# One transposing transfer of q issued from ScalarE's queue in place of SP's, in an attention and gated feed-forward kernel

## The chip, the cores and the metric

The kernel runs on one core of a Trainium2 chip. The engines that compute are TensorE (PE, whose weight loads are PEld), VectorE (DVE), ScalarE (ACT) and GpSimd (POOL); SyncE (SP) only issues transfers. Sixteen DMA engines move the data of all queues. The metric is the device time of one execution in microseconds (us), as the median of several.

## What is computed

For each of 8 batches and 8 heads, an attention without a score matrix, then a gated feed-forward over all 4608 tokens:

```
q_s = softmax(q, over the 64 channels)          # q, k, v: 8 x 8 x 576 x 64, float32
k_s = softmax(k, over the 576 positions)
kv  = k_s^T v                                    # 64 x 64 per head
x   = q_s kv                                     # all heads side by side: 4608 x 512
out = ((x w1) * (x w2)) w3 w_out                 # w1, w2: 512 x 1024; w3: 1024 x 1024; w_out: 1024 x 512
```

## The kernel before

Each batch is one round of attention, which prepares a chunk of 512 tokens of x, and one round of the feed-forward on that chunk; the 64 tokens left over of each batch make a ninth chunk. w3 and w_out are folded at the start into one matrix, W3O. The rounds are interleaved: while PE works on the feed-forward of chunk b, the other engines prepare the attention of the batches behind it.

Nothing orders the work at run time but semaphores. Each engine, and each engine's queue of transfers, takes its instructions in the order in which the program issued them, and that order is one long list of step names, `ORDER` (lines 77 to 164), written out by hand for all engines together. `Plan.run` (48 to 72) goes through it and calls each step's function; `attention` (521 to 797) and `chunk` define the steps, with the engine of each, what it needs and the time by which it was planned. A step's name ends in the batch and a part.

The steps that matter here:

- q of a batch comes in two parts, `PARTS` (298): p = 0 holds four blocks of 64 tokens, p = 1 five. For each part the softmax runs as `qmx` (maximum, DVE, L620), `qsub` (L625), `qexp` (ACT, L633), `qsm` (sum, DVE, L638), `qeps`, `qrc`, and `qn` (L657), which writes the normalized q in f16 into the tile `en`.
- `en` must be transposed into `qT` before PE can multiply it. Batch 0 and part 1 of batch 1 do that on PE (`qt`, L672, with evictions `qT`, L366). The others do it by a transfer, `qd` (L678 to 680): a transposing DMA from `en` to `qT`. `DMATP` (354) adds part 0 of batch 1 to these, so `qd.1.0` is the first such transfer of the run.
- `xm` (L705) multiplies `qT` by the kv matrix on PE; `xm.1.0` needs `qd.1.0`. `xs` evicts it to x (L370), and `up` (L851), `down` (L873) are the feed-forward.
- k of a batch: `kmx` (maximum, DVE, L532), `cba`, `cbx` (four small copies on ACT that exchange rows between groups of partitions, L545), `cb` (DVE, L549 and L551), `ksub` (L555), `kexp` (ACT, L563). `vc` casts v to f16 (L366). `kv` (PE, L580) needs both parts of `kexp` and of `vc`; `kve`, `kvr`, `kv2` finish it.

The loads come by two queues. Those of the weights and of the first batches are issued by POOL (`LOADS`, 252), those from q of batch 2 on by SP (`LATE`, 259; L450). The first of SP's late loads, `q.2`, waits until the load of w1's last part has landed. SP also issues all stores (L913, L1072) but for a few near the end, which ACT issues.

Around the change the order is, engine by engine:

- SP: `q.2`, `qd.1.0`, `v.2`, `k.3`, the stores of chunk 0.
- ACT: `bs.0.0.3`, `W3O.6`, `cbx.2`, `vc.1.1`, `kexp.1.0`, `vc.1.0`, `bs.0.1.3`, `os.0.1`, `kve.1`.
- POOL: `qn.1.0` comes before `ksub.1.0`, some steps earlier.
- PE: `down.0.0`, `up.0.0.1.3`, `down.0.1`, `kv.1`, `down.0.2`, `xm.1.0`, `down.0.3`.

Of the kernel before, what the change touches and what calls it, by code (L numbers as in the profile page):

```python
# [85 lines left out]
qsub.1.0 qexp.1.0 q.1.1 q.2 xts.0.0 bs.0.0.1 up.1.0.1.1 ab.0.1.0 cb.1 up.0.0.1.1 up.1.0.0.2 qsm.1.0  # L86
ksub.1.1 bs.0.1.1 ab.0.0.1 up.0.0.0.2 up.1.0.1.2 qeps.1.0 xts.0.1 qrc.1.0 qn.1.0 bs.0.0.2 ab.0.1.1
ab.0.0.2 kmx.2.0 cba.2 bs.0.1.2 kexp.1.1 up.0.0.1.2 up.1.0.0.3 up.0.0.0.3 up.1.0.1.3 bs.0.0.3 W3O.6
qd.1.0 cbx.2 ab.0.0.3 ksub.1.0 down.0.0 ab.0.1.2 cb.2 vc.1.1 kexp.1.0 vc.1.0 os.0.0 ksub.2.1
up.0.0.1.3 down.0.1 ksub.2.0 qmx.1.1 qsub.1.1 kv.1 bs.0.1.3 os.0.1 kve.1 kexp.2.1 kexp.2.0 ab.0.1.3  # L90
down.0.2 kvr.1 kv2.1 xm.1.0 down.0.3 xs.1.0.1 xs.1.0.0 up.1.1.0.0 up.0.1.0.0 up.1.1.0.1 qmx.2.1
qmx.2.0 os.0.2 qsub.2.1 qexp.1.1 bs.1.0.0 qsm.1.1 qsub.2.0 v.2 up.0.1.0.1 up.1.1.0.2 qexp.2.1
# [173 lines left out]
def kernel(  # L266
# [11 lines left out]
    nc = tc.nc  # L278
# [3 lines left out]
    P = 128  # L282
# [42 lines left out]
    st = {}  # L325
# [19 lines left out]

    EVICT = 100.0
    TWOQ = [7]
    SLACK = 0.0
    NX = 3
    DMATS = 1  # L350
# [5 lines left out]
    DMAT = [[b > DMATS or (b, p) in DMATP for p in range(2)] for b in range(B)]  # L356
# [21 lines left out]
    def pairs(n, pool=2.25):  # L378

        return {"POOL": (0.02 + n * pool / 1152.0, True), "DVE": (0.15 + n / 960.0, True)}  # L380
# [140 lines left out]
    def attention(b):  # L521
        kb, qb, vb = (inbuf[n][turn_of(n, b)] for n in "kqv")
        two = lambda hp: slice(2 * hp, 2 * hp + 2)
        old = b > 1
# [91 lines left out]
        def qmx(p):  # L616
            j = slice(*PARTS[p])
            if ("qm", b) not in st:
                st["qm", b] = work.tile([P, HH, NJ], F32, tag="qm", name="qm")
            dve.tensor_reduce(out=st["qm", b][:, :, j], in_=qb[:, :, j, :], axis=AX.X, op=ALU.max)  # L620

        def qsub(p, eng):
            j = slice(*PARTS[p])
            n = PARTS[p][1] - PARTS[p][0]
            return [engine[eng].tensor_tensor(  # L625
                out=qb[:, :, j, :], in0=qb[:, :, j, :],
                in1=st["qm", b][:, :, j, None].broadcast_to([P, HH, n, D]), op=ALU.subtract)]

        def qexp(p):
            j = slice(*PARTS[p])  # L630
            n = PARTS[p][1] - PARTS[p][0]
            st["eq", b, p] = work.tile([P, HH, n, D], F16, tag="eq", name="eq", bufs=4)
            nc.scalar.activation(out=st["eq", b, p], in_=qb[:, :, j, :], func=AF.Exp)  # L633

        def qsm(p):
            if ("qr", b) not in st:
                st["qr", b] = work.tile([P, HH, NJ], F32, tag="qr", name="qr")
            dve.tensor_reduce(out=st["qr", b][:, :, slice(*PARTS[p])], in_=st["eq", b, p],  # L638
                              axis=AX.X, op=ALU.add)

        def qeps(p, eng):
            rr = st["qr", b][:, :, slice(*PARTS[p])]
            if eng == "ACT":
                nc.scalar.activation(out=rr, in_=rr, func=AF.Identity, bias=epst[:, 0:1])
            else:
                return [dve.tensor_scalar_add(out=rr, in0=rr, scalar1=EPS)]

        def qrc(p):
            rr = st["qr", b][:, :, slice(*PARTS[p])]
            dve.reciprocal(out=rr, in_=rr)  # L650

        def qn(p, eng):
            j = slice(*PARTS[p])
            n = PARTS[p][1] - PARTS[p][0]
            if ("en", b) not in st:
                st["en", b] = work.tile([P, NJ, HH, D], F16, tag="en", name="en")
            return [engine[eng].tensor_tensor(  # L657
                out=st["en", b][:, j, :, :].rearrange("p j h d -> p h j d"), in0=st["eq", b, p],
                in1=st["qr", b][:, :, j, None].broadcast_to([P, HH, n, D]), op=ALU.mult)]

        def blocks(tile_, n0, n1):
            return tile_.rearrange("p j h d -> p (j h d)")[:, n0 * P:n1 * P]

        def qTt():
            if ("qT", b) not in st:
                st["qT", b] = work.tile([P, NJ * NHP, P], F16, tag="qT", name="qT")
            return st["qT", b]

        def qt(n0, n1):
            st["qtp", b, n0] = p_att([P, n1 - n0, P], F16, "qtp")  # L670
            for i in range(n0, n1):
                nc.tensor.transpose(st["qtp", b, n0][:, i - n0, :], blocks(st["en", b], i, i + 1),  # L672
                                    ident16)

        def qT(n0, n1, eng):
            copy(eng, qTt()[:, n0:n1, :], st["qtp", b, n0])

        def qd(p):  # L678
            n0, n1 = (x * NHP for x in PARTS[p])
            nc.sync.dma_start_transpose(out=qTt()[:, n0:n1, :], in_=blocks(st["en", b], n0, n1))  # L680

        def toks(i, hp, gg, j0, j1):

# [8 lines left out]
        def XRING(name):  # L692
            if name[1] < XMS:
                return "att"
            return "pab" if name[0] == "xt" else "po" if name[2] else "att"
# [20 lines left out]
        def A(*a, **kw):  # L716
            plan.add(*a, lead=A0, **kw)
# [5 lines left out]
        for hp in hps:  # L723
# [6 lines left out]
        A(("kv", b), "PE", 1.12 if VCAST[b] else 0.62, kv, [("kexp", b, hp) for hp in hps] +  # L730
          ([("v", b)] if VCAST[b] else [("vc", b, hp) for hp in hps]), takes="att", slots=2, slack=SLACK)
        A(("kve", b), "ACT", 0.47, kve, [("kv", b)])
        A(("kvr", b), "DVE", 0.25, kvr, [("kve", b)])
        A(("kv2", b), {"DVE": (0.6, False), "ACT": (1.0, False)}, 0, kv2, [("kvr", b)] + [("xt", b - 2)] * old, gives=[("kv", b)])
        for p in parts:
            n = (PARTS[p][1] - PARTS[p][0]) * HH * D
            A(("qmx", b, p), "DVE", 0.15 + n / 960, lambda p=p: qmx(p), [qin(p)])
            A(("qsub", b, p), pairs(n, 2.12), 0, lambda eng, p=p: qsub(p, eng), [("qmx", b, p)])
            A(("qexp", b, p), "ACT", 0.2 + n / 1200, lambda p=p: qexp(p), [("qsub", b, p)], takes="eq")
            A(("qsm", b, p), "DVE", 0.15 + n / 960, lambda p=p: qsm(p),  # L740
              [("qexp", b, p)] + [("qn", b - 2, x) for x in parts if old])
            A(("qeps", b, p), {"ACT": (0.31, False), "DVE": (0.18, True)}, 0,
              lambda eng, p=p: qeps(p, eng), [("qsm", b, p)])
            A(("qrc", b, p), "DVE", 0.26, lambda p=p: qrc(p), [("qeps", b, p)])
            A(("qn", b, p), pairs(n, 2.12), 0, lambda eng, p=p: qn(p, eng),
              [("qrc", b, p)] + QFREE(b - 2), gives=[("qexp", b, p)])
            n0, n1 = (x * NHP for x in PARTS[p])
            if DMAT[b][p]:
                A(("qd", b, p), "SP", 1.3, lambda p=p: qd(p), [("qn", b, p)] + [("xt", b - 2)] * old,
                  size=(n1 - n0) * P * P * 3)  # L750
            else:
                for m0 in range(n0, n1, 8):
                    m1 = min(m0 + 8, n1)
                    A(("qt", b, m0), "PE", 0.06 * (m1 - m0), lambda m0=m0, m1=m1: qt(m0, m1),
                      [("qn", b, p)], takes="att", slack=SLACK)
                    A(("qT", b, m0), {"ACT": (0.17 + (m1 - m0) * P / 1220, False),
                                      "DVE": (0.15 + (m1 - m0) * P / 1920, False)}, 0,
                      lambda eng, m0=m0, m1=m1: qT(m0, m1, eng), [("qt", b, m0)] + [("xt", b - 2)] * old, gives=[("qt", b, m0)])

        def qready(p):  # L760
            if DMAT[b][p]:
                return [("qd", b, p)]
            n0, n1 = (x * NHP for x in PARTS[p])
            return [("qT", b, m0) for m0 in range(n0, n1, 8)]
# [3 lines left out]
        if len(SUBS[b]) == 2:  # L768
            for h in range(2):
                name = ("xm", b, h)  # L770
                dst = lambda i, h=h: xtile()[:, i::2, h * 256:(h + 1) * 256]
                A(name, "PE", 0.22, lambda name=name, h=h: prod(name, [0, 1], 4 * h, 4 * h + 4, None),
                  kvs + qready(h) + free, takes=XRING(name), slots=2, slack=SLACK)
                for i in range(2):
# [5 lines left out]
        else:  # L780
            for hp in hps:
                name = ("xm", b, hp)
                A(name, "PE", 0.22, lambda name=name, hp=hp: prod(name, [hp], 0, NM, None),
                  kvs + qready(0) + qready(1) + free, takes=XRING(name), slots=2, slack=SLACK)
                for i in range(2):
# [6 lines left out]
        A(("xt", b), "PE", 0.07, lambda: prod(("xt", b), [0, 1], NM, NJ, None), last + qready(1),  # L792
          takes=XRING(("xt", b)), slots=2, slack=SLACK)
        for i in range(2):
# [39 lines left out]
    def QFREE(b):  # L834
        return [n for n in plan.steps if n[0] in ("qt", "qd") and n[1] == b]

    def chunk(c):
# [327 lines left out]
        if c in SEVEN:  # L1165
# [27 lines left out]
            for n, needs, gives in (  # L1193
# [4 lines left out]
                if n == 21 and c in FINE:  # L1198
# [10 lines left out]
                  needs + gone, gives=gives, takes=OSB)  # L1209
                if c in TWOQ:  # L1210
                    A(("sx", c, n), "ACT", 0.4, lambda n=n: store_block(n, z=1), [("os", c, n)],
                      gives=[("os", c, n)])
                A(("st", c, n), "SP", 1.15, lambda n=n: store_block(n, z=0 if c in TWOQ else None), [("os", c, n)],
                  gives=[("os", c, n)], size=P * C * 4)
# [46 lines left out]
    for c in range(B + 1):  # L1261
        if c < B:
            attention(c)
        chunk(c)
# [43 lines left out]
```

## Time and profile before

| | us |
|---|---|
| median of 3 runs | 230.85 (230.52 to 230.87) |
| the profiled execution | 231.41 |
| its span, from the first to the last instruction | 229.6 |
| PE busy in it | 220.3 |
| DVE, ACT, POOL busy | 202.6, 146.4, 144.1 |

The granted clock of TensorE was 1.0 of full speed throughout. A row of the timeline gives the start in us from the span's start, the time it took, the engine, the line of the kernel, the operation, the tile written and the tile read, and in brackets the time that the engine was idle just before and what ended it. SPq and ACTq are the issuing of a transfer by that engine, which is not counted as busy time; the transfer itself lands later. A row of the waits says who waited for whom, how long in total, how often, and the longest. A row of a stretch gives its length and then, for each engine in the order PE, PEld, DVE, ACT, POOL, the busy time and the instructions; at its end stand the granted clock, the busy share of the DMA engines and the GB/s that they moved.

### The profile page before, as it was taken

The page shows a single profiled execution, that of the slowest core. Times are in us where ns is not written, and L with a number is a line of the kernel's source. Part 1 is how long each engine was busy: PE and PEld are TensorE (multiplying, and loading weights), DVE is VectorE, ACT ScalarE, POOL GpSimd, SP SyncE. Part 2 cuts the span into 40 slices and gives each one's busy share as a digit, 9 for nine tenths or more (in the row PEclk, how much of TensorE's full clock was granted, in tenths as well). Part 3 has the DMA queues.
Part 4 walks back from the last instruction along what each step waited for, and adds up shares of the span by engine and source line. Part 5 has one row for each costly group of instructions (what it writes and reads, how often), then busy time and mean ns, then how long its engine had stood idle before and what let it go on. Part 6 is the DMA issues. An engine that isn't in the chain of part 4 may idle for free.

```text
span 229.6 us, 5583 instructions
## 1 busy us (share of the span) xinstructions
PE 220.3 (96%) x2239; PEld 149.1 (65%) x2239; DVE 202.6 (88%) x313; ACT 146.4 (64%) x277; POOL 144.1 (63%) x93
## 2 busy tenths in 40 slices
PE   7789999999999999999999999999999999999993
PEld 2345658765857635345665665664788788888882
DVE  1997769989897999999999899899989999899982
ACT  0536865479964899968947889448578453344521
POOL 8233337909999987994895895643099335638200
PEclk9999999999999999999999999999999999999999
DMA  6999999999999979999892866872803430041537
GB/s 201 219 310 210 294 264 264 312 382 295 394 311 215 358 259 222 283 302 301 246 386 76 179 139 176 330 150 47 183 3 76 97 74 1 3 91 27 113 91 229
DMA packets 42201, 46.56 MB, mean 203 GB/s; under 512 B 17088, under 2 KB 29888, under 8 KB 42176
## 3 DMA queue, kind: packets, MB, share of 16 engines
q1 hardware_dynamic: 33920, 33.82, 53.0%
q0 software_dynamic: 7536, 11.73, 21.8%
q10 hardware_dynamic: 720, 0.66, 1.0%
q8 instruction: 17, 0.28, 0.5%
q14 instruction: 8, 0.07, 0.1%
HBM read 38.80 MB, written 9.44 MB: 210 GB/s over the span
## 4 chain that ended last, share of the span: by engine, by line
PE 72%; DMA 22%; issue 1%; POOL 1%; ACT 1%; DVE 0%; POOLq 0%; ACTq 0%
PE pab L851 27%; PE po L1029 16%; PE pg L939 9%; PE pab L939 7%; DMA q<-in_q_dram 6%; DMA k<-in_k_dram 6%; PE po L873 6%; DMA w1sb<-in_moe_w_dram 5%; DMA v<-in_v_dram 4%; PE pab L1029 2%; PE pkv L580 2%; PE xm L705 1%; POOL w L450 1%; PE po L705 0%; POOL wosb L450 0%
## 5 line engine op out<-in xcount | busy, mean ns | idle before, releaser
L851 PE MATMUL pab<-x,w1sb 128*128 128x256 f16 (+1 forms) x256 | 49.5, 326 | 0.3 <-DMA w1sb<-in_moe_w_dram 0.3
L851 PE MATMUL pab<-x,w2sb 128*128 128x256 f16 (+1 forms) x256 | 49.5, 326 | 0.0
L555 POOL TENSOR_TENSOR k<-k,cb 128x1152 f32<-128x1152 f32 x13 | 34.1, 2634 | 14.7 <-DVE w L1008 8.6
L851 PEld LDWEIGHTS <-w1sb 128*128 128x128 f16 x256 | 24.5, 98 | 15.1 <-DMA w1sb<-in_moe_w_dram 0.6
L851 PEld LDWEIGHTS <-w2sb 128*128 128x128 f16 x256 | 24.2, 98 | 15.2 <-issue 1.1
L866 DVE TENSOR_TENSOR ab<-pab,bsb 128x512 f16<-128x512 f32 x48 | 31.8, 676 | 2.0 <-ACT bsb L366 1.2
L625 POOL TENSOR_TENSOR q<-q,qm 128x1280 f32<-128x1280 f32 (+1 forms) x13 | 27.8, 2144 | 4.8 <-issue 2.3
L366 ACT CAST bsb<-pab 128x512 f16<-128x512 f32 x37 | 21.7, 585 | 12.6 <-PE pab L851 12.1
L657 POOL TENSOR_TENSOR en<-eq,qr 128x1024 f16<-128x1024 f16 (+1 forms) x12 | 25.4, 2124 | 6.5 <-ACT bsb L366 5.0
L620 DVE TENSOR_REDUCE qm<-q 128x20 f32<-128x1280 f32 (+1 forms) x16 | 21.3, 1339 | 3.9 <-DMA q<-in_q_dram 3.9
L638 DVE TENSOR_REDUCE qr<-eq 128x20 f32<-128x1280 f16 (+1 forms) x16 | 21.5, 1341 | 1.6 <-ACT eq L633 1.5
L633 ACT ACTIVATE eq<-q 128x1280 f16<-128x1280 f32 (+1 forms) x16 | 18.6, 1167 | 5.3 <-DVE q L625 3.9
L1029 PEld LDWEIGHTS <-w 128*128 128x128 f16 x192 | 18.6, 98 | 4.1 <-issue 0.4
L532 DVE TRANSPOSE_TENSOR_REDUCE kt<-k 128x72 f32<-128x2304 f32 x8 | 20.6, 2570 | 0.1
L366 ACT COPY q<-pg 128x512 f32<-128x512 f32 x19 | 10.8, 586 | 13.9 <-PE pg L939 7.7
L1029 PEld LDWEIGHTS <-ab 128*128 128x128 f16 x168 | 16.4, 98 | 3.5 <-issue 0.2
L563 ACT ACTIVATE ek<-k 128x1152 f16<-128x1152 f32 x16 | 18.3, 1165 | 0.0
L1029 PE MATMUL po<-w 128*128 128x256 f16 x144 | 18.0, 273 | 0.0
L1008 POOL TENSOR_TENSOR w<-ab 128x1024 f16<-128x1024 f16 x5 | 10.6, 2125 | 9.7 <-PE pg L939 3.7
L501 PE MATMUL po<-wosb,w3T 128*128 128x512 f16 x64 | 15.3, 379 | 0.6 <-DMA wosb<-in_moe_w_out_dram 0.5
L873 PE MATMUL po<-W3O,ab 128*128 128x512 f16 x64 | 15.1, 379 | 0.5 <-ACT osb L366 0.5
L366 ACT CAST v<-v 128x1152 f16<-128x1152 f32 x12 | 13.6, 1156 | 2.0 <-DMA v<-in_v_dram 2.0
(145 smaller groups left out, 425.2 us busy)
## 6 DMA issues: line engine op xcount, KB each, us to landing
out_dram<-osb SPq DMA_DIRECT2D x56, 128.0 KB, 2.6
q<-in_q_dram SPq DMA_DIRECT2D x5, 1152.0 KB, 8.0
v<-in_v_dram SPq DMA_DIRECT2D x5, 1152.0 KB, 7.2
k<-in_k_dram SPq DMA_DIRECT2D x4, 1152.0 KB, 9.5
k<-in_k_dram POOLq DMA_DIRECT2D x3, 1152.0 KB, 14.3
v<-in_v_dram POOLq DMA_DIRECT2D x1, 1152.0 KB, 14.0
q<-in_q_dram SPq DMA_DIRECT2D x2, 576.0 KB, 5.8
k<-in_k_dram SPq DMA_DIRECT2D x2, 576.0 KB, 5.0
```

The lines of the kernel that those rows point to most:

```text
L366: return [(nc.scalar.copy if eng == "ACT" else engine[eng].tensor_copy)(out=out, in_=in_)]
L532: dve.tensor_reduce(out=st["kt", b].rearrange("p h j e -> p (h j e)"), in_=kb.rearrange("p h j (e c) -> p (h j e) c", c=QD), axis=AX.X, op ...
L555: return [engine[eng].tensor_tensor(out=kb[:, two(hp), :, :], in0=kb[:, two(hp), :, :], in1=st["cb", b][:, two(hp), None, :].broadcast_to( ...
L620: dve.tensor_reduce(out=st["qm", b][:, :, j], in_=qb[:, :, j, :], axis=AX.X, op=ALU.max)
L625: return [engine[eng].tensor_tensor(out=qb[:, :, j, :], in0=qb[:, :, j, :], in1=st["qm", b][:, :, j, None].broadcast_to([P, HH, n, D]), op ...
L638: dve.tensor_reduce(out=st["qr", b][:, :, slice(*PARTS[p])], in_=st["eq", b, p], axis=AX.X, op=ALU.add)
L657: return [engine[eng].tensor_tensor(out=st["en", b][:, j, :, :].rearrange("p j h d -> p h j d"), in0=st["eq", b, p], in1=st["qr", b][:, :, ...
L851: nc.tensor.matmul(st["p", one, c, sub, u][:, a * (t1 - t0):(a + 1) * (t1 - t0)], lhsT=w[:, ct, fb * P:(fb + 1) * P], rhs=x()[:, ct, t0:t1 ...
L866: dve.tensor_tensor(out=st["ab", c][:, nf * u:nf * u + nf, t0:t1], in0=cut(st["p", 0, c, sub, u]), in1=cut(st["bsb", c, sub, u]), op=ALU.mult)
L873: nc.tensor.matmul(st["po", c, tb], lhsT=st["ab", c][:, ft, tb * P:(tb + 1) * P], rhs=W3O[:, ft, :], start=(ft == 0), stop=(ft == N_FT - 1))
L939: nc.tensor.matmul(st["pg", one, c, g, bank][:, a * 256:a * 256 + 256], lhsT=t[:, c0 + ct, f:f + P], rhs=r[:, r0 + ct, t0:t0 + 256], start ...
L1029: nc.tensor.matmul(to, lhsT=t[:, f0 + ft, t0 + tb * P:t0 + tb * P + P], rhs=r[:, g0 + ft, c0:c0 + 256], start=fresh and (tb == 0 or wide_) ...
```

## The change

The transfer `qd.1.0` is issued by ACT and not by SP. In `ORDER` a new step, `qa.1.0`, stands just ahead of `qd.1.0`, that is, on ACT between `W3O.6` and `cbx.2`; it issues the transfer. `qd.1.0` stays as an empty step, so that what needed it (`xm.1.0`) still needs it. On SP the transfer is gone and `v.2` follows `q.2` directly. The other twelve transposing transfers stay on SP.

```diff
-qd.1.0 cbx.2 ab.0.0.3 ksub.1.0 down.0.0 ab.0.1.2 cb.2 vc.1.1 kexp.1.0 vc.1.0 os.0.0 ksub.2.1
+qa.1.0 qd.1.0 cbx.2 ab.0.0.3 ksub.1.0 down.0.0 ab.0.1.2 cb.2 vc.1.1 kexp.1.0 vc.1.0 os.0.0 ksub.2.1
...
     TWOQ = [7]
+    ASIDE = [(1, 0)]
...
         def qd(p):
             n0, n1 = (x * NHP for x in PARTS[p])
-            nc.sync.dma_start_transpose(out=qTt()[:, n0:n1, :], in_=blocks(st["en", b], n0, n1))
+            (nc.scalar if (b, p) in ASIDE else nc.sync).dma_start_transpose(
+                out=qTt()[:, n0:n1, :], in_=blocks(st["en", b], n0, n1))
...
-            if DMAT[b][p]:
+            if DMAT[b][p] and (b, p) in ASIDE:
+                A(("qa", b, p), "ACT", 1.3, lambda p=p: qd(p), [("qn", b, p)] + [("xt", b - 2)] * old)
+                A(("qd", b, p), "SP", 0.02, lambda: None, [("qa", b, p)], size=(n1 - n0) * P * P * 3)
+            elif DMAT[b][p]:
                 A(("qd", b, p), "SP", 1.3, lambda p=p: qd(p), [("qn", b, p)] + [("xt", b - 2)] * old,
                   size=(n1 - n0) * P * P * 3)
```

## The prediction

> **What bounds the kernel now.** I read the page first: TensorE (PE) is busy for 220.3 of 229.6 us and carries most of the chain that ended last.
>
> ```profile
> span 229.6 us, 5583 instructions
> PE 220.3 (96%) x2239; PEld 149.1 (65%) x2239; DVE 202.6 (88%) x313; ACT 146.4 (64%) x277; POOL 144.1 (63%) x93
> PE 72%; DMA 22%; issue 1%; POOL 1%; ACT 1%; DVE 0%; POOLq 0%; ACTq 0%
> ```
>
> So an edit counts only if it makes PE wait, or removes a wait of PE. The waits of PE from 44 us to the end (columns: total us, times, longest) are four short ones:
>
> ```profile
> PE po L873 <- ACT osb L366: 0.5, 1, 0.5
> PE pab L851 <- DMA w1sb<-in_moe_w_dram: 0.3, 1, 0.3
> PE xm L705 <- DMA qT<-en: 0.3, 1, 0.3
> PE po L1029 <- ACT x L370: 0.2, 1, 0.2
> ```
>
> The one on w1sb lies before the change. That leaves 0.5 + 0.3 + 0.2 = 1.0 us that could be gained at all, and no limit on what could be lost. Next I read the place of the change: the timeline of SP, where L680 is the moved transfer (qd.1.0) and the other lines are loads, and the row of POOL that makes its input.
>
> ```profile
> 45.88 0.37 SPq L450 DMA_DIRECT2D q<-in_q_dram  x1
> 46.30 3.63 SPq L680 DMA_TRANSPOSE qT<-en  x1
> 50.04 0.52 SPq L450 DMA_DIRECT2D v<-in_v_dram  x1
> ...
> 41.88 1.90 POOL L657 TENSOR_TENSOR en<-eq,qr 128x1024 f16<-128x1024 f16 x1
> ```
>
> The input is ready at 41.88 + 1.90 = 43.78. The transfer goes out at 46.30 only because the load of q of batch 2 (q.2) stands ahead of it on SP. And it holds SP for 3.63 us, so that the load of v of batch 2 (v.2) leaves at 50.04. Now ScalarE (ACT), which is to issue it behind the eviction of W3O.6 (L370, 46.03) and ahead of cbx.2 (L545), then vc.1.1, kexp.1.0, vc.1.0:
>
> ```profile
> 46.03 0.60 ACT L370 ACTIVATE W3O<-po 128x512 f16<-128x512 f32 x1
> 46.68 0.82 ACT L545 COPY mx<-mx 32x8 f32<-32x8 f32 x4
> 48.82 1.15 ACT L366 CAST v<-v 128x1152 f16<-128x1152 f32 x1 [1.33 <-DMA v<-in_v_dram]
> 49.88 1.16 ACT L563 ACTIVATE ek<-k 128x1152 f16<-128x1152 f32 x1
> 50.95 1.14 ACT L366 CAST v<-v 128x1152 f16<-128x1152 f32 x1
> ```
>
> and PE on its chain in the same stretch:
>
> ```profile
> 50.38 1.73 PE po L873 x8
> 52.13 0.77 PE pkv L580 x71
> ...
> 54.74 0.03 issue
> 54.77 0.41 PE xm L705 x8
> ```
>
> Two things are tight. The second cast of v ends at 50.95 + 1.14 = 52.09 and kv.1 (L580), which reads it, starts at 52.13 just as PE comes free (50.38 + 1.73 = 52.11): whatever delays ACT from 48.82 on delays PE by as much. And xm.1.0 (L705), which reads the transposed q, starts at 54.77 as PE comes free at 54.74. When the transfer lands stands in the answer for its line in this stretch, and below it that for the whole run:
>
> ```profile
> DMA to landing us min/median/max: 8.3/8.3/8.3
> ...
> L680 SPq DMA_TRANSPOSE qT<-en x13: 1231/1348/3631, 46.3 to 174.2; - x13
> DMA to landing us min/median/max: 3.1/3.7/8.3
> ```
>
> It lands at 46.30 + 8.3 = 54.6, 0.14 us before PE wants it. Ahead of both stands the one gap of this stretch: ACT idles 1.33 us before 48.82 for the load of v of batch 1.
>
> **What the change does, part by part.**
>
> *ACT gains the issue of one transposing transfer.* Its wait on POOL is over by 43.78, so it adds no waiting. How early can ACT's queue start it, and does it hold the engine? The stores that ACT issues near the end show that:
>
> ```profile
> 214.67 0.58 ACT L366 COPY kept<-po 128x512 f32<-128x512 f32 x1 [0.29 <-PE po L1029]
> 214.74 0.72 ACTq L1072 DMA_DIRECT2D out_dram<-k  x1
> 215.50 0.58 ACT L366 CAST spare<-pg 128x512 f16<-128x512 f32 x1 [0.24 <-issue]
> L1072 ACTq DMA_DIRECT2D out_dram<-k x3: 602/607/720, 214.7 to 221.8; - x3
> L1072 SPq DMA_DIRECT2D out_dram<-k x3: 595/595/596, 213.4 to 221.5; - x3
> ```
>
> The issue starts 0.07 us after the instruction ahead of it started, runs beside it, and the next one follows 0.04 us after the issue ends (214.74 + 0.72 = 215.46, then 215.50). ACT takes about as long over such a store as SP (607 against 595 ns). So qa.1.0 starts at about 46.03 + 0.07 = 46.10.
>
> Its length is the unknown. No row shows a transposing issue on ACT. The nearest are SP's 13: least 1.23, median 1.35, most 3.63, and the 3.63 is this very one. I take 1.35. Two rows argue for it:
>
> ```profile
> 85.81 1.26 SPq L680 DMA_TRANSPOSE qT<-en  x1
> 84.00:86.00 2.00, 2.00 (x11) 0.78 (x8) 2.00 (x3) 2.00 (x4) 2.00 (x2) 1.00 1.03 362
> 127.21 2.14 SPq L680 DMA_TRANSPOSE qT<-en  x1
> ```
>
> At 85.81 the DMA engines are as full (share 1.03, last two columns) as at 46, and the issue takes 1.26. What differs at 46.30 is that q.2 was put on the same queue 0.42 us before (45.88, above) and has hardly begun to move: I read the 3.63 as SP's queue having no room behind it. ACT's queue is empty then. Against it: 46.30 is also the first such issue of the run, and 2.14 at 127.21 shows that other causes add 0.8 us.
>
> With 1.35 the issue ends at 47.45. cbx.2 (0.82) runs from 47.50 to 48.32 in place of 46.68 to 47.50, still 0.50 us before the v that the next cast waits for. Its result goes to VectorE (DVE), which transposes it (L551) and then waits for PE:
>
> ```profile
> 48.41 0.45 DVE L551 STREAM_TRANSPOSE cb<-mxe 128x256 f32<-128x256 f32 x1
> 49.54 0.69 DVE L366 COPY osb<-po 128x512 f32<-128x512 f32 x1 [0.69 <-PE po L873]
> ```
>
> DVE can start on it at 48.32, 0.1 us ahead of that row's start, so it moves by 0.1 us at most, inside the 0.69 us that DVE waits for PE anyway. Cost of the ACT side: 0. The cover is gone once the issue exceeds 48.82 - 0.82 - 0.05 - 46.10 = 1.85 us; from there each microsecond is one of PE. The ends of this term: 0 and 3.63 - 1.85 = 1.8 us.
>
> *SP loses 3.63 us of issue.* v.2 goes out at about 46.3 in place of 50.04. k.3 needs the exponential that ends at 49.88 + 1.16 = 51.04, so it and the stores behind it stay. v.2 is first read here, with no idle time before it, so its coming early is worth nothing:
>
> ```profile
> 60.23 1.14 ACT L366 CAST v<-v 128x1152 f16<-128x1152 f32 x1
> ```
>
> *The transfer changes its place among the DMAs.* Its issue is 0.2 us earlier at most; what it gains or loses is its turn. These are the queues from 46.2 to 50 (q0 POOL's loads, q1 SP's), the DMA in two stretches (last column GB/s), and the loads of v that SP issues:
>
> ```profile
> q0 software_dynamic: 219, 0.93, 65.5%
> q1 hardware_dynamic: 218, 0.50, 36.3%
> ...
> 52.00:54.00 2.00, 1.97 (x79) 1.33 (x79) 1.90 (x5) 1.98 (x6) 2.00 (x1) 1.00 0.89 151
> 62.00:67.00 5.00, 5.00 (x109) 3.49 (x106) 4.90 (x12) 3.69 (x8) 5.00 (x3) 1.00 1.05 398
> ...
> v<-in_v_dram SPq DMA_DIRECT2D x5, 1152.0 KB, 7.2
> ```
>
> Until now it stands in one queue behind q.2 (45.88) and ahead of v.2. On its own queue it need not wait for q.2, but v.2 may overtake it. Bounds for its landing: early, as a median one, 46.10 + 3.7 = 49.8, worth nothing since PE comes at 54.74; late, behind all of v.2, 1152 KB (1.18 MB) at 398 GB/s = 3.0 us after 54.6, that is 57.6, which costs 57.6 - 54.74 = 2.9 us. I take a landing between 51 and 54.7, at no cost, since it is issued almost as early as q.2 and is small (128 x 1024 f16 is 256 KB, where q.2 has the 1152 KB of a v).
>
> The Trainium skill ("DMA: Bandwidth & Descriptors", Queues, rings and completion order) says that each DMA engine goes round-robin between the queues with work, packet by packet. By that rule two queues would share each engine, and the transfer of small packets would be held back by every large packet of q.2 and v.2; the rows above, where q0 and q1 both move data, agree that queues overlap but do not show the turn.
>
> *Sum:* 0 (ACT) + 0 (SP) + 0 (landing) = 0. The profiled execution took 231.41 us, of which 1.81 lie around its span of 229.6; it is 0.56 above the median of the runs, 230.85, so the difference that the sum gives is added to that median. Forecast: 230.9.
>
> **The rivals.**
>
> *The issue is as long on ACT as on SP* (slower). If the 3.63 us came from full DMA engines or from a first use, ACT is held to 49.73, cbx.2 ends at 50.60, the casts and kv.1 follow 1.8 us late: 232.6. It decides from 1.85 us on. For it: the only row at this moment is 3.63. Against: the row at 85.81, and the median of 1.35.
>
> *The transfer lands late* (slower). v.2 goes first on the DMA engines, and PE waits at xm.1.0 (a wait that no row has now): at most 2.9 us, by half shares 1.4, so 232.3 (to 233.7). For it: only 0.14 us of slack, and no row that shows whose turn comes first. Against: the transfer is issued ahead of v.2's data, 0.2 us behind q.2. The Trainium skill's rule above leads to this case.
>
> *The DMA backlog shrinks* (faster). From 52 to 54 the DMA moves 151 GB/s, where it moves 398 from 62 to 67: a hole of 2 x (1 - 151/398) = 1.2 us. It lies just before the transposing transfer lands (54.6), with v.2 behind it in the same queue. If v.2 moves on a queue of its own the hole may fill, and the traffic queued up to 67 ends about a microsecond earlier. Two of PE's waits come from that traffic: 0.3 for the next qT, and 0.5 for an eviction behind a cast of v that waited:
>
> ```profile
> 79.26 1.16 ACT L366 CAST v<-v 128x1152 f16<-128x1152 f32 x1 [0.63 <-DMA v<-in_v_dram]
> ```
>
> Both gone: 0.8 us, so 230.1. Against: that the DMA engines could go on with v.2 while the transposing transfer has its turn is shown by no row.
>
> **Chances.** Hidden on all sides 0.38 (230.6 to 231.2); long issue 0.22; late landing 0.16; shorter backlog 0.24. Faster or slower by over 0.2% (0.46 us) is about what measurement can tell here, the three runs lying within 230.52 to 230.87. So faster 0.24, same 0.38, slower 0.38. The range takes in the backlog case whole, the long issue, and the late landing to two thirds of its price: 230.0 to 232.8; the rest of that case is what is left out.
>
> **What would show it.** Right: L680 on ACT near 46.1, about 1.35 us long; cbx.2 ending before 48.8; kv.1 near 52.13, xm.1.0 near 54.77; v.2 issued near 46.3. Wrong: an issue on ACT over 1.85 us with an idle "issue" before L545 and kv.1 late; or PE waiting at xm for DMA qT; or the cast at 48.82 later because v landed later; on the other side, the waits of 0.3 at xm and 0.5 at the eviction gone.

## The result, and the profile after it

| us | before | after |
|---|---|---|
| median of 4 runs each, same chip | 230.80 (230.52 to 230.87) | 237.95 (236.94 to 238.13) |
| the profiled execution | 231.41 | 236.94 |
| its span | 229.6 | 235.1 |
| granted clock of PE, mean over the span | 1.0 | 0.993 |

The changed kernel takes 1.0296 times as long, with a 95% interval of 1.0272 to 1.032: 3% slower, and 5 us beyond the upper end of the range. The profiled execution is the shortest of the four, 1.0 us below their median. Lines of the program have moved by a few: L705 is now L707, L851 is L856, L873 is L878, L366 is L367, and the moved transfer is issued at L681.

The page of the changed kernel first, with the busy times of the engines.

```profile
span 235.1 us, 5584 instructions
PE 220.9 (94%) x2239; PEld 149.2 (63%) x2239; DVE 203.0 (86%) x313; ACT 146.1 (62%) x277; POOL 144.0 (61%) x93
```

PE does as much as before, with the same count of products; the 5.5 us are not work. Its waits from 44 us on (total us, times, longest) say where they are:

```profile
PE xm L707 <- DMA qT<-en: 5.1, 1, 5.1
PE pab L856 <- DMA w1sb<-in_moe_w_dram: 0.3, 1, 0.3
PE po L1034 <- ACT x L371: 0.2, 1, 0.2
```

One new wait of 5.1 us, at xm.1.0, for the very transfer that was moved. Now the timeline at the change: ACT, then SP, then PE.

```profile
45.57 0.58 ACT L367 CAST bsb<-pab 128x512 f16<-128x512 f32 x1
45.58 1.37 ACTq L681 DMA_TRANSPOSE qT<-en  x1
...
48.85 1.15 ACT L367 CAST v<-v 128x1152 f16<-128x1152 f32 x1 [1.04 <-DMA v<-in_v_dram]
...
45.83 0.37 SPq L451 DMA_DIRECT2D q<-in_q_dram  x1
46.29 0.45 SPq L451 DMA_DIRECT2D v<-in_v_dram  x1
51.10 0.37 SPq L451 DMA_DIRECT2D k<-in_k_dram  x1
...
52.17 0.77 PE L581 MATMUL pkv<-v,ek 64*64 64x65 f16 x72
59.87 0.64 PE L707 MATMUL xm<-qT,kv 64*64 64x256 f16 x8 [5.10 <-DMA qT<-en]
60.44 3.00 PE L878 MATMUL po<-W3O,ab 128*128 128x512 f16 x8
```

The issue on ACT takes 1.37 us from 45.58, and what PE waits for on ACT stays in place: the cast of v starts at 48.85 (48.82 before), kv.1 at 52.17 (52.13). The transfer is even issued ahead of q.2 (45.83). Yet the chain of waits follows it for 14.15 us:

```profile
45.58 14.15 DMA qT<-en
```

It lands at 59.7 where before it landed at 54.6. The DMA queues show what happens in all that time. These are packets, MB and share of the 16 engines from 45.5 to 48, from 48 to 50, from 50 to 57 and from 57 to 59.8; q0 is POOL's, q1 SP's, q10 ACT's.

```profile
q0 software_dynamic: 225, 1.01, 103.4%
...
q1 hardware_dynamic: 207, 0.48, 70.0%
...
q10 hardware_dynamic: 64, 0.02, 4.9%
...
q1 hardware_dynamic: 880, 1.96, 87.2%
q10 hardware_dynamic: 876, 0.22, 22.8%
...
q1 hardware_dynamic: 237, 0.54, 92.7%
q10 hardware_dynamic: 116, 0.02, 24.3%
```

Until 48 neither new queue moves a packet: POOL's loads come first, as before. From 50 to 57 ACT's queue gets 876 packets through and SP's 880, one for one, and in each single microsecond of that stretch the two counts lie within 4 of each other, but for the last with 155 to 149. But a packet of the transfer is 0.22 MB / 876 = 250 bytes and one of a load 1.96 MB / 880 = 2,200. So a queue of small packets that takes turns with a queue of large ones gets a tenth of the bytes. By the landing, 207 + 880 + 237 = 1,324 load packets have gone. Before, with the transfer behind q.2 in one queue, q.2 alone went ahead (1.18 MB, 512 of these packets). The difference, 0.48 + 1.96 + 0.54 - 1.18 = 1.80 MB, takes 4.5 us at 398 GB/s (an estimate), of the 5.1 us by which the transfer is later. The Trainium skill ("DMA: Bandwidth & Descriptors", Queues, rings and completion order) states this turn, round-robin between queues at packet granularity; 876 to 880 agrees with it. Its packet typically holds several descriptors; whether that is what the profile counts as a packet, no run here shows.

The same stretch in windows (length, PE, PEld, DVE, ACT, POOL, clock, DMA share, GB/s) shows a second thing and a third. First two windows while the transfer is on its way, then three around PE's return:

```profile
54.50:55.50 1.00, 0.27 (x2) 0.00 (x0) 1.00 (x1) 1.00 (x1) 1.00 (x1) 1.00 1.31 147
57.00:58.50 1.50, 0.00 (x0) 0.00 (x0) 0.33 (x1) 0.00 (x0) 1.50 (x1) 1.00 1.27 76
...
59.00:59.50 0.50, 0.00 (x0) 0.00 (x0) 0.00 (x0) 0.00 (x0) 0.50 (x1) 0.81 1.07 290
61.00:62.00 1.00, 1.00 (x4) 0.30 (x2) 0.00 (x0) 1.00 (x3) 0.71 (x1) 0.50 1.06 398
62.50:63.00 0.50, 0.50 (x3) 0.25 (x2) 0.17 (x1) 0.30 (x1) 0.00 (x0) 0.78 0.23 86
```

At 54.5 and at 57 the DMA engines are taken (share 1.31 and 1.27; above 1, more than one packet per engine is under way) and move 147 and 76 GB/s: packets are held, not missing. Between 54 and 60 a load packet takes 0.09 us as a median and up to 1.36 us. And PE, when it starts again, has half its clock, from 59.3 to 62.7 (0.81 and 0.78 are the windows in which it falls and rises). What that costs shows beside the kernel before, whose PE went on without a stop:

```profile
55.12 1.90 PE L873 MATMUL po<-W3O,ab 128*128 128x512 f16 x8
56.85 1.04 PE L851 MATMUL pab<-x,w2sb 128*128 128x256 f16 x8
```

From xm.1.0 to the next `up` it took 56.85 - 54.77 = 2.08 us; now it takes 3.41, since `up` starts at 63.28:

```profile
63.28 0.93 PE L856 MATMUL pab<-x,w2sb 128*128 128x256 f16 x7
```

The sum is 5.10 (wait) + 1.33 (half clock) - 0.76 (the two later waits of before, 0.3 and 0.5, which are gone) = 5.7, against 5.5 us of span.

### The profile page after: what moved, and what is told of

It reads as the page before. It is cut to its first block, busy times and chain, and to the rows that moved or that the text cites. A ratio compares the mean times of both kernels' runs of the same rounds, so it can differ in the third digit from the quotient of the medians.

```text
span 235.1 us, 5584 instructions
## 1 busy us (share of the span) xinstructions
PE 220.9 (94%) x2239; PEld 149.2 (63%) x2239; DVE 203.0 (86%) x313; ACT 146.1 (62%) x277; POOL 144.0 (61%) x93
## 4 chain that ended last, share of the span: by engine, by line
PE 79%; DMA 13%; POOL 4%; DVE 1%; issue 1%; ACT 0%; POOLq 0%
PE pab L856 31%; PE po L1034 16%; PE pg L944 9%; PE pab L944 7%; DMA w<-in_moe_w_dram 7%; DMA qT<-en 6%; PE po L878 4%; PE po L502 4%; PE pab L1034 2%; PE pkv L581 2%; POOL k L556 2%; PE xm L707 1%; PE w3t L490 1%; POOL w L451 1%; POOL en L658 1%
## 5 line engine op out<-in xcount | busy, mean ns | idle before, releaser
L856 PE MATMUL pab<-x,w1sb 128*128 128x256 f16 (+1 forms) x256 | 49.5, 326 | 0.3 <-DMA w1sb<-in_moe_w_dram 0.3
L856 PE MATMUL pab<-x,w2sb 128*128 128x256 f16 (+1 forms) x256 | 49.5, 326 | 0.0
L856 PEld LDWEIGHTS <-w1sb 128*128 128x128 f16 x256 | 24.5, 98 | 15.0 <-DMA w1sb<-in_moe_w_dram 0.5
L856 PEld LDWEIGHTS <-w2sb 128*128 128x128 f16 x256 | 24.3, 98 | 15.1 <-issue 1.1
L367 ACT CAST bsb<-pab 128x512 f16<-128x512 f32 x37 | 21.7, 586 | 14.0 <-PE pab L856 13.7
L367 ACT COPY q<-pg 128x512 f32<-128x512 f32 x19 | 10.8, 586 | 14.0 <-PE pg L944 7.7
L878 PE MATMUL po<-W3O,ab 128*128 128x512 f16 x64 | 16.3, 401 | 0.0
L371 ACT ACTIVATE x<-xm 128x512 f16<-128x512 f32 x18 | 10.2, 600 | 8.6 <-PE xm L707 8.5
```

What stands on the lines that cost most here:

```text
L367: return [(nc.scalar.copy if eng == "ACT" else engine[eng].tensor_copy)(out=out, in_=in_)]
L856: nc.tensor.matmul(st["p", one, c, sub, u][:, a * (t1 - t0):(a + 1) * (t1 - t0)], lhsT=w[:, ct, fb * P:(fb + 1) * P], rhs=x()[:, ct, t0:t1 ...
L878: nc.tensor.matmul(st["po", c, tb], lhsT=st["ab", c][:, ft, tb * P:(tb + 1) * P], rhs=W3O[:, ft, :], start=(ft == 0), stop=(ft == N_FT - 1))
```

## The experiments

Three theories. **A, turns:** packets alternate between two queues that both have work, so a transfer of small packets on a queue of its own is slowed by large loads on the other. **B, the issuer:** a transposing transfer is slow because ACT issues it. **C, bytes ahead:** it only waits for the bytes of v.2, which now leaves early. Ratios are to the kernel before, on the same chip; where an experiment is set against the changed kernel, the two were not run together, and the kernel before took 230.80 beside the one and 230.82 to 231.07 beside the others. A diff shows the main lines of an experiment, with dots for what stands between them; a step that moves in `ORDER` is gone from its old place.

**1. v.2 waits for the transfer.** The change, with v.2 issued only after the transfer has landed; q.2 is beside it as before.

```diff
+            if name == ("v", 2):
+                tc.add_manual_dep(st[name].ins, st["moved"].ins.name, ...)
...
+            if (b, p) in ASIDE:
+                st["moved"] = d
```

> The transfer stays on ACT's queue, and the load v.2 on SP waits until it has landed. Theory A (the DMA engines take a packet of ACT's queue and a packet of SP's queue by turns, so each of the transfer's 64 packets per engine pays for one big load packet): only the 32 packets of q.2 per engine are left to take turns with, the rest of the transfer runs alone, it lands near 55 in place of 59.8, and PE waits 0 to 1 us at xm.1.0 in place of 5.1; median 231 to 232. Theory B (a transposing transfer is slow when ACT issues it, whatever else runs): it still lands past 58, PE waits over 4 us, median 236 or more. Theory C (only the bytes of v.2 that go ahead of it count): lands near 55 too, so this run tells A and C from B.

Measured: 234.59 (233.91 to 237.19) against 231.07, ratio 1.0176 (1.0117 to 1.0235). Waits, landing and one window of the profiled execution:

```profile
PE xm L714 <- DMA qT<-en: 4.5, 2, 3.5
...
DMA to landing us min/median/max: 12.5/12.5/12.5
...
50.00:53.00 3.00, 3.00 (x46) 1.73 (x48) 2.53 (x3) 3.00 (x4) 0.72 (x1) 1.00 0.86 52
```

Without v.2 the kernel is 3.4 us faster than the changed one, so v.2 is a large part. But the transfer, issued at 46.2, still landed at 58.7 in this execution, 3.5 us late with no byte of v.2 ahead of it: v.2's bytes are not the whole cause, as C has it, and the number of A (the same 55) was missed too. Nor were there turns at first: from 48 to 50 the transfer got 431 packets through and q.2 11. Then, for 3 us, the DMA moved 52 GB/s with little but q.2 and the transfer: a stall of the kind seen above, worth 3 x (1 - 52/398) = 2.6 us. The profiled execution is the longest of the four, the others were 2.5 to 3.3 us shorter.

**2. The transfer third in SP's queue.** The kernel before, with the order q.2, v.2, `qd.1.0` on SP.

```diff
-qd.1.0 cbx.2 ...
+v.2 qd.1.0 cbx.2 ...
```

> From the kernel before: the transfer stays on SP's queue but is issued after v.2, so all of q.2 and v.2 go ahead of it in one queue. Theory C (it is the bytes of q.2 and v.2 ahead of it): it lands as late as in the changed kernel, near 59.8, with the same 5 us of waiting. Theory A: in one queue there are no turns, it is served at full rate once v.2 is through; v.2 is 1.18 MB, 3.0 us at 398 GB/s, so it lands near 54.6 + 3 = 57.6, earlier than on the queue of its own, and PE waits about 2.9 us; median near 234. Theory B: PE waits nothing beyond those 3 us either.

Measured: 236.91 (236.56 to 237.43) against 231.07, ratio 1.0257 (1.0238 to 1.0277).

```profile
46.46 6.05 SPq L680 DMA_TRANSPOSE qT<-en  x1
...
DMA to landing us min/median/max: 12.1/12.1/12.1
```

It landed at 58.6, and PE waited 4.3 us. Standing behind both loads in one queue is about as bad as taking turns with both. The 58.6 lies between what A and C named, so it does not decide between them; the time is 2.9 us above the 234 that A gave. The issue held SP for 6.05 us, with two loads ahead, in place of 3.63 with one.

**3. The roles exchanged.** The kernel before, with v.2 issued by ACT right after `qd.1.0` in `ORDER`, the transfer on SP behind q.2.

```diff
-                st[name] = (nc.sync if queue == "SP" else g_).dma_start(
+                st[name] = (nc.scalar if name == ("v", 2) else nc.sync if queue == "SP" else g_).dma_start(
```

> From the kernel before: the transfer stays on SP's queue right behind q.2; v.2 is issued from ACT's queue at the time at which the changed kernel issues the transfer there. Theory A: now q.2 and then the transfer take turns packet by packet with v.2, of equal size to q.2; q.2 needs twice its time, about 6 us from 48 to 54, and the transfer follows with hardly anything left beside it: it lands near 57, PE waits 2 to 3 us, median 233 to 234. Theory B (ACT's queue is slow for transposing transfers only): the transfer lands at 54.6 or earlier, median 230.8.

Measured: 236.71 (236.41 to 239.32) against 231.07, ratio 1.0272 (1.0217 to 1.0327).

```profile
DMA to landing us min/median/max: 14.5/14.5/14.5
...
q10 hardware_dynamic: 363, 0.84, 69.6%
q1 hardware_dynamic: 362, 0.67, 55.2%
...
54.00:56.50 2.50, 1.08 (x6) 0.29 (x3) 0.56 (x3) 1.97 (x2) 2.50 (x2) 1.00 0.98 83
```

Issued by SP, the transfer takes 14.5 us when the other queue carries a load: B falls. It landed at 61.2, past the 57 of A, and PE waited 6.2 us, in a profiled execution that is 2.4 us longer than any of the other three. From 50 to 54 the queues are again served one for one, 363 to 362, most of them load packets on both. And again there is a stall, 83 GB/s over 2.5 us. The issue held SP for 6.30 us behind q.2 alone, which now moved at half its rate: the time goes with how long what stands ahead takes to move.

**4. Another transfer on ACT, at a quiet time.** `qd.1.0` back on SP; `qd.7.0` issued by ACT, with `qa.7.0` ahead of it in `ORDER`.

```diff
-    ASIDE = [(1, 0)]
+    ASIDE = [(7, 0)]
```

> From the kernel before: qd.1.0 stays on SP; another transposing transfer of the same size, part 0 of batch 7, which lands 3.1 us after its issue near 160 us, when no load is under way, is issued from ACT in its place. Theory A (turns with load packets, and stalls of the DMA engines' step): nothing to take turns with, it lands 3 to 3.5 us after its issue; median within 0.3 of before. Theory B (ACT's queue is slow for it as such): it lands 6 us or more after its issue.

Measured: 231.11 (230.73 to 231.40) against 230.90, ratio 1.0003 (0.9985 to 1.002).

```profile
162.37 1.37 ACTq L681 DMA_TRANSPOSE qT<-en  x1
...
qT<-en ACTq DMA_TRANSPOSE x1, 3.2
```

It landed 3.2 us after its issue (3.1 in the kernel before, on SP). A transposing transfer issued by ACT is as quick as one issued by SP where no large load stands beside it: B falls a second time.

**5. The transfer first in SP's queue.** The kernel before, with `qd.1.0` ahead of q.2.

```diff
-qd.1.0 cbx.2 ...
+qd.1.0 q.2 cbx.2 ...
```

> From the kernel before: the transfer stays on SP's queue but is issued ahead of q.2, at 43.8. Theory A with stalls: in one queue there are no turns; the DMA engines come free from POOL's loads between 48 and 50.2 and the transfer needs the last of them, so it lands between 51.5 and 52.5, two to three us earlier than the 54.6 of before; PE does not wait for it. q.2 and v.2 follow about as late as before, since the engines' waiting for each other only moves from 52 to 54 forward to 48 to 50. Median within 0.5 of before, more likely a little lower. The opposite (q.2 lands 1 us or more later and the maxima behind it hold PE) would give 231.5 to 232.5.

Measured: 231.23 (230.66 to 231.67) against 230.90, ratio 1.0006 (0.999 to 1.0023).

```profile
43.65 1.33 SPq L680 DMA_TRANSPOSE qT<-en  x1
...
DMA to landing us min/median/max: 8.0/8.0/8.0
...
52.00:54.00 2.00, 1.92 (x79) 1.24 (x78) 1.83 (x3) 1.93 (x6) 2.00 (x1) 1.00 1.07 396
```

It landed at 51.7, three microseconds earlier than before, and the time is the same. The hole at 52 to 54 was filled (396 GB/s where before had 151), but another opened ahead of it: 192 and 257 GB/s from 48 to 50 and from 50 to 52, where before had 369 and 356. It moved, as expected, and did not go. With nothing ahead of it in its queue the issue took 1.33 us, not 3.63.

**6. Loads in smaller packets.** The change, with q.2, v.2 and k.3 each loaded as two transfers of half the columns, so that a packet has half the bytes.

```diff
+            m = cols // 2 if name in [("q", 2), ("v", 2), ("k", 3)] else cols
...
-                    out=dst[:, x:x + n], in_=src[:, x:x + n])
+                    out=dst[:, x:x + n, y:y + m], in_=src[:, x:x + n, y:y + m])
```

> The changed kernel, but q.2, v.2 and k.3 are each issued as two transfers of half the columns, so that their packets have 1152 bytes in place of 2304; bytes, queues and order are as in the changed kernel. Theory A: a turn costs half as much, so the transfer's 64 turns per engine end after q.2 in place of after q.2, v.2 and a part of k.3: it lands 3 to 5 us earlier, at 55 to 57, and PE waits 0.3 to 2.3 us; median 231.5 to 234.5. Theories B and C: no packet size enters, PE waits 5 us again, median near 238.

Measured: 232.69 (232.11 to 233.31) against 231.07, ratio 1.0064 (1.0041 to 1.0088). Landing, and the two queues from 48 to 50 and from 50 to the landing:

```profile
DMA to landing us min/median/max: 9.4/9.4/9.4
...
q1 hardware_dynamic: 437, 0.49, 71.1%
q10 hardware_dynamic: 125, 0.03, 7.0%
...
q1 hardware_dynamic: 644, 0.73, 64.4%
q10 hardware_dynamic: 931, 0.23, 58.1%
```

The same bytes are asked for by the same queues (v.2 between 47.07 and 49.11 in place of 46.29), and the transfer lands at 55.6, four microseconds earlier; the kernel is 5.3 us faster. By the landing 437 + 644 = 1,081 load packets and 125 + 931 = 1,056 of the transfer have gone. The sums are about one for one, and the load packets now carry 1.22 MB, about what q.2 alone carried ahead of it before. Landing and time are those that A named. But the way there was not all turns: from 50 to 50.5 the transfer got 306 packets through and the loads 30, and from 50 to 54 the DMA moved only 137 to 140 GB/s. Splitting also doubles the number of transfers, which this run doesn't separate.

**7. q.2 and v.2 behind the transfer.** The change, with q.2 waiting for the landing too.

```diff
+            if name == ("q", 2):
+                tc.add_manual_dep(st[name].ins, st["moved"].ins.name, ...)
...
-qa.1.0 qd.1.0 cbx.2 ...
+qa.1.0 qd.1.0 q.2 cbx.2 ...
```

> The changed kernel, but q.2 on SP, and with it v.2, waits until the transfer on ACT's queue has landed: beside it there are only POOL's loads up to 50.2. Theory A with stalls: it waits for the last DMA engine and then runs at full rate, landing at 51.5 to 53 in place of 59.8, with no wait of PE at xm.1.0; but q.2 lands about 4 us later than before, at 57 to 58, and may hold DVE and then PE: median 231 to 234. Theory B: it lands past 56.

Measured: 234.43 (234.18 to 236.31) against 230.90, ratio 1.0163 (1.0121 to 1.0206).

```profile
DMA to landing us min/median/max: 5.6/5.6/5.6
...
DVE qm L626 <- DMA q<-in_q_dram: 4.3, 1, 4.3
PE pab L863 <- DVE ab L878: 2.5, 1, 2.5
...
65.00:66.00 1.00, 1.00 (x66) 0.87 (x57) 1.00 (x3) 1.00 (x3) 0.87 (x2) 0.50 1.03 408
```

With no load on SP's queue the transfer on ACT lands 5.6 us after its issue instead of 14.2, at 51.3, and PE does not wait at xm: B falls here too. The other half of the trade shows too: q.2, issued at 51.35, makes DVE wait 4.3 us and through it PE 2.5, with the half clock once more; the time is 0.4 us above the range expected.

**8. PE kept busy.** The change, with 18 products of zeros on PE ahead of xm.1.0, which nothing reads.

```diff
-    "begin": 17, "pf.5.0": 6,
+    "begin": 17, "pf.5.0": 6, "xm.1.0": 18,
```

> The changed kernel with 18 matrix products on zeros, which nothing reads, ahead of xm.1.0 in PE's order: about 4 us of work inside the 5.1 us in which PE waits. If the granted clock of 0.5 for 3.4 us after that wait comes from PE's idling, it stays at 1.0, the products behind the wait run at full speed and the median falls by 1.0 to 1.7, to 236.3 to 237. If the clock has another cause, the median stays near 238.

Measured: 235.80 (235.45 to 236.29) against 230.90, ratio 1.0207 (1.0173 to 1.024); 2.15 us less than the changed kernel, and 0.5 us below the range expected.

```profile
54.79 4.05 PE L394 MATMUL po<-spare 128*128 128x512 f16 x18
60.40 0.41 PE L707 MATMUL xm<-qT,kv 64*64 64x256 f16 x8 [1.56 <-DMA qT<-en]
60.74 1.90 PE L878 MATMUL po<-W3O,ab 128*128 128x512 f16 x8
```

The transfer is as late as ever (xm.1.0 at 60.40), but `down` takes 1.90 us and not 3.00, and the clock stays at 1.0. Part of the loss was PE's clock, and work that does nothing wins it back. It won more than the 1.33 us of the profiled execution; two of the three other runs of the changed kernel had a mean clock of 0.985, which is about two such spells, not one.

**9. Loads in quarter packets.** As 6, with four transfers each; the first line below is that of 6.

```diff
-            m = cols // 2 if ...
+            m = cols // 4 if ...
```

> The changed kernel, but q.2, v.2 and k.3 are each issued as four transfers of a quarter of the columns: packets of 576 bytes in place of 2304. It landed at 59.8 with whole packets and at 55.6 with halves. Theory A (turns packet by packet, plus stalls): a turn costs half of that with halves again, 64 of them about 2 us less, so the transfer lands at 53 to 54.5 and PE's wait at xm.1.0 goes; the median falls below that with halves (232.7) by up to 0.8, unless the more numerous issues on SP make k.3 and the stores late. If only the stalls count and not the turns, it lands near 55.6 again.

Measured: 238.21 (237.43 to 238.89) against 230.82, ratio 1.0322 (1.0273 to 1.0371).

```profile
51.38 1.39 ACTq L683 DMA_TRANSPOSE qT<-en  x1
52.81 0.82 ACT L548 COPY mx<-mx 32x8 f32<-32x8 f32 x4 [5.92 <-issue]
53.66 1.15 ACT L367 CAST v<-v 128x1152 f16<-128x1152 f32 x1
```

Inconclusive on packet size: the edit added a wait. With more transfers on SP, the semaphore on which the transfer's landing is counted (113 in both records) was one that q.2's first quarter used, and ACT waited for that quarter until 51.3 before it could issue. The run is useful for another step: ACT's cast came 4.84 us late (53.66 against 48.82) and kv.1 on PE as late (56.97 against 52.13).

## Why the prediction was wrong

- *PE bounds the kernel, 1.0 us to gain, no limit to lose.* Right: the loss is one wait of PE and what it did to PE's clock.
- *The issue on ACT takes about 1.35 us and is hidden.* Right: 1.37 us in the change and in experiment 4. It started at 45.58, 0.5 us before the forecast, beside the cast ahead of W3O.6. The rival "as long on ACT as on SP" falls: the 3.63 us belong to the place behind q.2 (1.33 with nothing ahead, though the first such issue of the run there too; 6.05 behind two loads), which fits the reading of "no room behind it". One row was misread, at no cost: DVE reads the result of cbx.2 first in L549, at 48.22, and not in L551; the shift stays 0.1 us. Experiment 9 bears out the rule that ACT's delay from the cast on is PE's, one for one.
- *SP is free earlier and v.2 leaves at about 46.3; worth nothing.* The time was right (46.29). But v.2 landed no earlier for it: 13.2 us later, at 59.5, where before it landed 8.9 us after 50.04, at 58.9. It was costed as v.2's gain alone, and what it did was put a second 1.18 MB into the queue with which the transfer takes turns.
- *The landing "between 51 and 54.7, at no cost".* This is the step that failed: it landed at 59.7, and PE waited 5.1 us. The reason given, that the transfer is issued almost as early as q.2 and is small, counts bytes and order of issue. From 50 on the engines served packets by turns: about 1,000 small ones, nearly each paired with a load packet nine times as large. Being issued first gained nothing either: its first packet went at 49.25, a microsecond behind the first of q.2 at 48.20. The row was there (0.14 us of slack), and the turn was named as a rival's support, and yet the likely value was taken from size.
- *The late bound, 57.6.* Too early by 2.1 us. It let v.2 go ahead whole and stopped there; but by the landing 1,324 load packets had gone, 300 more than q.2 and v.2 have together, so k.3 (issued at 51.10) took turns as well. 300 x 2,304 bytes at 398 GB/s are 1.7 us. The rest (0.4 us) is of the size of the stalls, whose lost time in the two windows is estimated at 1.0 x (1 - 147/398) + 1.5 x (1 - 76/398) = 1.8 us, less the hole that before had as well (1.2).
- *The price of a late landing.* It was put at the wait alone, 2.9 us at most. Missing was the half clock that a PE idle for 5 us comes back with: 1.33 us in the profiled execution, 2.15 between the medians with and without the products of experiment 8. The rival "transfer lands late" was thus right in its kind and place (a wait at xm for qT), with 0.16 of the chance and less than half the price.
- *The rival "backlog shrinks".* Its signs came (the waits of 0.3 and 0.5 were gone), most likely only since everything behind xm.1.0 was later. Whether a shorter backlog is worth anything stays untested: in experiment 5 the hole at 52 to 54 was filled, but one of about its size opened from 48 to 52.

Shown: the loads in the other queue make the transfer late (1, 7), whoever issues it (3, 4), and less so when they are split into smaller packets (6); that half the clock was part of the loss (8). Read from two traces, the changed kernel's and that of experiment 8 (892 load packets to 864 from 50 to 57): the one-for-one turns, whose load packets make, by the estimate above, most of the 5.1 us. Open: why the engines hold packets for 1 to 3 us at 52 to 147 GB/s. Each such stretch read here had the transposing transfer under way; its cause was not tested. Nor is it settled how much of the lateness such stalls make in another execution: by turns alone experiment 1 should have landed near 55 and not at 58.7, experiment 3 near 57 and not at 61.2, so there the stalls seem to do more than the turns. No version tried here beats the kernel before.

## What to carry to other kernels

A second queue is no private lane: here the 16 engines served SP's and ACT's queues packet by packet, and the transfer of small packets took longer beside a queue of large ones (14.2 us) than behind one load in the same queue (8.3) or first in it (8.0, experiment 5). When an issue is moved off a queue, list what that queue now sends earlier and ask what it will run beside. And price a new wait of PE of several microseconds with the slow clock behind it, not with the wait alone.

## What the runs showed of the hardware that was not expected

- *PE's clock.* After 5.1 us of idling it was 0.5 for 3.4 us, after the 2.5 us wait of experiment 7 as well (PE idle from 60.96 to 63.42, clock 0.5 from 64.2, when PE had been back for 0.8 us, to 67.6); after the 1.56 us left in experiment 8 it stayed at 1.0. The Trainium skill ("TensorE: Matmul & The Clock Gate", Part 1) gives about 3.4 us both for the idling that drops the clock and for the work that restores it. The second agrees with the 3.4 us here; the first is longer than the 2.5 that sufficed, and the measurement decides.
- *POOL's loads held the others back.* From 45.5 to 48 neither q1 nor q10 moved a packet, though both had transfers issued by 45.83; POOL's loads took 103% of the engines. The first packets came at 48.20 (q.2) and 49.25 (the transfer), 2.4 and 3.7 us after the issues. With the engines free of other loads the start took 1.0 us for q.2 (experiment 7) and 1.3 us for a transposing transfer (experiment 4). One-for-one turns with POOL's queue were not seen.
- *Transfers of different queues can share a semaphore*, so that a transfer on ACT waits for a load on SP to land (experiment 9: semaphore 113, 5.92 us of ACT).
